# Filling products that go on up to the up projection of the third and fourth chunks, in the scores' bank; a chunk's w loaded by itself; planner keys set anew

## The chip, the cores and the metric

The kernel runs on one core of one Trainium2 chip. The metric is the time of one execution on the device, in microseconds. Five engines matter here: PE (matrix products), DVE (VectorE), ACT (ScalarE), POOL (GpSimd) and SP, which in this kernel issues nearly all transfers between HBM and SBUF. Each engine works through its own instructions in the order written; waits between engines are semaphores.

## What is computed

The first half is a linear attention with decay (RWKV-6) over 4 batches, 8 heads, 768 steps and a head size of 48. The second half is a projection up from 384 to 2048 columns, a gate, and a projection down to 384, over 3072 tokens.

```python
for t in range(S):
    cur = einsum('bhd,bhe->bhde', u * kt, vt)
    y[:, :, t] = einsum('bhd,bhde->bhe', rt, state + cur)
    state = wt[..., None] * state + einsum('bhd,bhe->bhde', kt, vt)
x = y.transpose(0, 2, 1, 3).reshape(3072, 384)
h = x @ w_in                                # 384 -> 2048
out = (h * clip(h + 3, 0, 6) / 6) @ w_out   # 2048 -> 384
```

## The kernel before

**Chunks and blocks.** The sequence is cut into chunks of 128 steps (`L`), 24 in all, numbered in the order in which they are worked on. Four chunks make a block of 512 tokens, of which there are six. For a chunk `i`, VectorE runs two scans over the decays w (`back{i}`, line 372, and `fore{i}`, line 381), from which `K{i}` (392) and `R{i}` (396) are made. PE forms the scores (`score{i}`, line 440, into the PSUM banks bankB and bankC) and transposes K (`turn{i}`, 456). `above{i}` (447, VectorE) takes the scores out of both banks. The product of K and v (`kv{i}`, 536) feeds the state by way of `kvs{i}` (ScalarE, 543), `mid{i}` (477), `decb{i}` (469) and `state{i}` (485). A chunk's own term, r times k times u, is made on VectorE and PE for the first `BY_PE` chunks (`own{i}` 405, `dot{i}` 415, `sum{i}` 421), and on GpSimd and VectorE for the others (408, 423), which need one more load (`rkt{i}`).

In the first block the result of a chunk is read in two pieces, `first{i}` (lines 514 and 523) and, after ScalarE's `third{i}` (576), `read{i}` (584, 514, 523); ScalarE's `leave{i}` (594, 596) brings it to `xT`. The up products of that block are `up0.f.c0` (line 639): f counts 16 groups of 128 of the 2048 columns. For the first four groups (`CUT`) the block is cut in two, so `up0.0.0` to `up0.3.0` need chunks 0 and 1 alone, and `up0.0.2` to `up0.3.2` need chunks 2 and 3. The others take all four chunks at once. They alternate between bankC and bankA. `ramp` (629, ScalarE) and `gate` (650, VectorE) empty the bank. `down0...` (658, 791) follow, and then the later blocks, with their products in seven-product form (740, 791).

**Weights.** w_in and w_out arrive as 64-bit floats, and are made into 32-bit ones in the kernel, in sixteen pairs: `fetch{j}` loads pair j (line 331, 768 KB), ScalarE's `low{j}` and `whole{j}` (340, 344) and VectorE's `shift{j}`, `join{j}` and `full{j}` (349, 354, 359) convert it. Three buffers hold what is loaded, and a buffer is free again when `low{j}` and `join{j}` have read it.

**Order.** The order on each engine is made by a planner (`Plan.order`, line 110), while the kernel is built: each step has an engine, an assumed duration, the steps it needs, the ring buffers it holds and a key, the time it is due. Of the steps that can start first on an engine, the one with the smallest key is taken. `START` gives the keys of chunks 0 to 5, `CONV` those of the weights, and `BEHIND[i]` names the weight load after which a chunk's loads are issued. The order of SP is made in the same way. SP issues a load only when the buffer for it is free, and all later loads wait behind it.

**Filling products.** `Plan.emit` (line 174) writes the instructions in that order. Ahead of a PE step that by the plan starts later than the one before it ended, it puts products whose result nobody reads: `spin` (line 1133), identity by two copies of identity, 128 rows by 128 by 256 columns, as many as fill 0.75 of the planned gap (`FILL`) at 0.43 us each (`SPIN`). They write bankA, of which there are two, and end with the first up product, `until = "up0.0.0"`.

Of the kernel before, what the change touches and what calls it, by code (L numbers as in the profile page):

```python
# [18 lines left out]
L = 128  # L19
# [8 lines left out]
LAG = 19.7  # L28
AHEAD = -3.5
LEAD = 7.0  # L30
BEHIND = (-1, -1, 1, 3, 8, 7)
BY_PE = 10
OWN = -0.17
SOLO = (0, 2, 3, 4, 5)
EARLY = 11
START = (-108.3, -118.2, -107.0, -152.7, 31.1, 13.0)
CONV = (-100.6, 6.9)
UP = (-64.2, 3.9, -40.1, 4.9)
SUMS = (54.2, 0.9)
LEAST = 2.0 ** -60  # L40
# [42 lines left out]
class Plan:  # L83
# [9 lines left out]
    spin = until = None  # L93
# [94 lines left out]
def fast_path(tc, feat, tok, wflat, ub, ug, moe_w_in, moe_w_out, out, flag, n_chunks):  # L188
# [5 lines left out]
    nc = tc.nc  # L194
# [13 lines left out]
    f64 = moe_w_in.dtype != F32  # L208

    with ExitStack() as ctx:  # L210
# [8 lines left out]
        chunk_of = [(i // NSEQ * 2 + i % 2) * n_chunks + i % NSEQ // 2 for i in range(NT)]  # L219

        def is_first(i):
            return i % NSEQ < 2

        def is_last(i):
            return i % NSEQ >= NSEQ - 2

        plan = Plan()
        st = [dict() for _ in range(NT)]
        blocks = [dict() for _ in range(NB)]


        ident = const.tile([128, 128], F32, name="ident")
# [4 lines left out]
        back = const.tile([PR, 2 * P, HL + 1], F32, name="back")  # L237
        starts = [const.tile([PR, 2 * P, HL + 1], F32, name=f"start_{i}") for i in range(2)]
        states = [const.tile([PR, P, D], F32, name=f"state_{i}") for i in range(2)]
        u_col = const.tile([PR, P, 2], F32, name="u_col")  # L240
# [37 lines left out]
        n = P * L  # L278
# [3 lines left out]

        def load_feat(i):
            a = io.tile([PR, nf], F32, name="feat_in")
            if i == 0:
                nc.sync.dma_start(out=a[:, 2 * n:], in_=feat[chunk_of[i], :, 2 * n:])
                nc.scalar.dma_start(out=u_col, in_=ug)
            else:
                nc.sync.dma_start(out=a, in_=feat[chunk_of[i]])
            st[i].update(a=a, r=a[:, :n].rearrange("q (x t) -> q x t", t=HL),  # L290
                         k=a[:, n:2 * n].rearrange("q (x t) -> q x t", t=HL), w=a[:, 2 * n:])

        def load_rest():
            nc.sync.dma_start(out=st[0]["a"][:, :2 * n], in_=feat[chunk_of[0], :, :2 * n])

        def load_u():
            nc.sync.dma_start(out=u_bc, in_=ub.to_broadcast([128, HD]))
# [103 lines left out]
        def own(i):  # L401
            d = st[i]
            if i < BY_PE:
                d["rk"] = wk.tile([PR, P, L], F32, name="rk", bufs=1)
# [12 lines left out]
        def own_sum(i):  # L417
            d = st[i]
            d["dg"] = wk.tile([L, H, 1], F32, name="dg")
            if i < BY_PE:  # L420
                nc.scalar.copy(out=d["dg"].rearrange("s h o -> s (h o)"), in_=d["dg_ps"].rearrange("s p g -> s (p g)"))
# [209 lines left out]
        def bank(name):  # L631
            return pp.tile([128, 512], F32, name=name, bufs=1 if name == "bankB" else 2)
# [234 lines left out]
        def do(fn, *args):  # L867
            return lambda: fn(*args)
# [5 lines left out]
        def when(i):  # L874

            bk, c = divmod(i, BC)
            return BASE[bk] - LAG - (BASE[bk] - BASE[bk - 1]) / BC * (BC - 1 - c) if bk else -99.0
# [11 lines left out]
        def scored(i):  # L889
            return f"score{i}" if i <= BC else f"read{i - 1}"  # L890

        def turned_by(i):
            return f"turn{i}" if i <= BC + 1 else f"begin{i - 2}"

        def written_by(i):
            return f"kv{i}" if i in SOLO else f"read{i - 1 if i <= BC else i - 2}"

        for i in range(NT):
            t = when(i)
            k = START[i] if i < len(START) else when(i - 2) - AHEAD  # L900
            first, last = is_first(i), is_last(i)
            dve = i < EARLY
            behind = [f"fetch{BEHIND[i]}"] if i < len(BEHIND) and BEHIND[i] >= 0 else []
            plan.add(f"feat{i}", "SP", 0.45 if i else 1.15, do(load_feat, i), behind + [f"feat{i - 1}"] * (i > 0) + ["later"] * (i == 1), k - 20, kb=690 if i else 231,
                     hold=[("feat", [f"K{i}", f"R{i}"] + [f"own{i}"] * (i < BY_PE))])
            plan.add(f"tok{i}", "SP", 0.45, do(load_tok, i), behind + [f"feat{i}"] * (i > 1) + ["later"] * (i < 2), k - 19.9, kb=197,
                     hold=[("tok", [f"read{i}"])])
            if i >= BY_PE:
                plan.add(f"rkt{i}", "SP", 0.45, do(load_rk, i), behind + [f"feat{i}"] * (i > 0), k - 19.8, kb=393,
                         hold=[("rk_in", [f"own{i}"])])  # L910
            plan.add(f"back{i}", "DVE", 1.4, do(back_scan, i), [f"feat{i}"] + [f"fore{i - 2}"] * (i > 1) + [f"back{i - 1}"] * (i > 0), k,
                     [("E", [f"K{i}", f"least{i}"])], port=True)
            plan.add(f"K{i}", "DVE" if dve else "POOL", 0.66 if dve else 1.32, do(make_k, i), [f"back{i}", f"least{i}"] + [f"K{i - 1}"] * (i > 0) + ["later"] * (i == 0),
                     k + 0.1, [("K", [scored(i), turned_by(i)])], port=True)
            plan.add(f"fore{i}", "DVE", 1.23, do(fore_scan, i), [f"back{i}"] + [f"fore{i - 1}"] * (i > 0), k + 0.2,
                     [("W", [scored(i), f"read{i}" if i < BC else f"begin{i}"])], port=True)
            plan.add(f"R{i}", "DVE" if dve else "POOL", 0.66 if dve else 1.32, do(make_r, i), [f"fore{i}"], k + 0.3,
                     port=True)
            plan.add(f"least{i}", "ACT", 0.2, do(least, i), [f"back{i}"], k + 0.2)
            if i < BY_PE:  # L920
                plan.add(f"own{i}", "DVE", 0.66, do(own, i), [f"feat{i}"] + ["later"] * (i == 0) + [f"own{i - 1}"] * (i > 0), k + OWN,
                         [("rk", [f"dot{i}"])], port=True)
                plan.add(f"dot{i}", "PE", 0.85, do(own_dot, i), [f"own{i}"], k + OWN, [("ps", [f"sum{i}"])])
                plan.add(f"sum{i}", "ACT", 0.22, do(own_sum, i), [f"dot{i}"], k + OWN, [("dg", [f"diag1{i}"])])
            else:
                plan.add(f"own{i}", "POOL", 2.0, do(own, i), [f"rkt{i}", "u"] + [f"own{i - 1}"] * (i > 0), k + 0.4,
                         [("rk", [f"sum{i}"])], port=True)
                plan.add(f"sum{i}", "DVE", 0.54, do(own_sum, i), [f"own{i}"], k + 0.5, [("dg", [f"diag1{i}"])])
            plan.add(f"diag0{i}", "ACT", 1.0, do(diagonal, i, 0), [f"sum{i}"] + [f"diag1{i - 1}"] * (i > 0), k + 0.6, [("A", [f"read{i}"])])
            plan.add(f"diag1{i}", "ACT", 1.0, do(diagonal, i, 1), [f"sum{i}", f"diag0{i}"], k + 0.6)  # L930
            due = k + 0.7 if i < len(START) else when(i - 1)
            t = k + 1 if i < len(START) else t
            if i <= BC:
# [7 lines left out]
            if i in SOLO:  # L941
                plan.add(f"kv{i}", "PE", 0.5, do(write_alone, i), [f"turned{i}", f"tok{i}"], t - 0.2, [("y", [f"kvs{i}"])])
            plan.add(f"kvs{i}", "ACT", 0.48, do(written, i), [written_by(i)], t - 6 if i >= len(START) else t - 0.5,
                     [("kvs", [f"decb{i}"] if last else [f"state{i}"])])
            S_ = [("S", [f"read{i}" if i < BC else f"begin{i}"] + [f"state{i}"] * (not last))]
            if not first:
                plan.add(f"decay{i}", "DVE" if dve else "POOL", 0.35 if dve else 1.0, do(decay, i),
                         [f"state{i - 2}", f"least{i}"] + [f"decay{i - 1}"] * (not is_first(i - 1)), t - 0.1 if i < len(START) else t - 5, S_, port=True)
                plan.add(f"mid{i}", "DVE", 0.3, do(middle, i), [f"kvs{i}", f"decay{i}"], t - 0.1 if i < len(START) else t - 5,
                         port=True)  # L950
# [34 lines left out]
                                 [f"leave{i - 1}", f"leave{i}"], when(i) - 50, kb=1, dmas=3)  # L985

        plan.add("u", "SP", 0.45, load_u, ["fetch3"], -60.0, kb=197)
        plan.add("later", "SP", 0.45, load_rest, ["feat0"], key=-999.0, kb=459)

        for j in range(len(pairs)):  # L990
            t = CONV[0] + j * CONV[1]
            plan.add(f"fetch{j}", "SP", 0.45, do(fetch, j), ["later"] * (j == 0), key=t - 20, kb=768 if f64 else 384,
                     hold=[("bits", [f"low{j}", f"join{j}"])] if f64 else ())
            if f64:
                plan.add(f"low{j}", "ACT", 0.9, do(low_scaled, j), [f"fetch{j}"], t, [("more", [f"full{j}"])])
                plan.add(f"whole{j}", "ACT", 0.84, do(low_whole, j), [f"low{j}"], t)
                plan.add(f"shift{j}", "DVE", 0.56, do(high_shift, j), [f"fetch{j}"], t, [("top", [f"full{j}"])], port=True)
                plan.add(f"join{j}", "DVE", 0.96, do(high_join, j), [f"shift{j}"], t, port=True)
                plan.add(f"full{j}", "DVE", 0.94, do(high_low, j), [f"join{j}", f"whole{j}"], t, port=True)
# [4 lines left out]
        for f in range(NFC):  # L1004
            for x, (c0, c1) in enumerate(parts(f)):
                m = c1 - c0
                at = 0 if m < BC and x == 0 else 2
                k = UP[at] + f * UP[at + 1]
# [7 lines left out]
        for c in classic:  # L1016
            for q in range(HF):
                k = D0 + c * D0 / BC + q * 1.29
# [33 lines left out]
        for bk in range(NB):  # L1052
            K = BASE[bk]
# [5 lines left out]
            for q in range(HF * (bk > 0)):  # L1059
# [13 lines left out]
                for what, eng, after, key in (("s1", "ACT", [u + "1"], 1), ("v", "ACT", [u + "5"], 2), ("u", "ACT", [u + "6"], 5),  # L1073
# [4 lines left out]
                    if q == 0 and what in ("s1", "v"):  # L1078
                        p = 0 if what == "s1" else 1
# [41 lines left out]
        for k, (which, j) in enumerate(vets):  # L1121
            i = 8 + k // 2
# [8 lines left out]
        plan.add("end", "PE", 0.0, lambda: None, [f"down{NB - 1}.1.{k_}.1" for k_ in range(1, 8)], BASE[NB])  # L1131

        def spin():
            nc.tensor.matmul(bank("bankA").rearrange("p (n t) -> p n t", t=L)[:, :2], lhsT=ident,  # L1134
                             rhs=ident.rearrange("p (n t) -> p n t", n=1).to_broadcast([128, 2, L]), start=True, stop=True)

        plan.spin, plan.until = spin, "up0.0.0"
        constants()
        plan.emit()

# [334 lines left out]
```

## Time and profile before

| | |
|---|---|
| median of 13 runs | 578.3 us (574.98 to 580.32) |
| profiled execution | 578.38 us, of which its span 576.6 us |
| mean granted PE clock | 0.983 |
| PE busy | 561.1 us (97%), 5508 products in the records |
| DVE, ACT, POOL busy | 408.3, 272.3, 84.5 us |
| records of line 1134 (fillings) | 42, from 1.4 to 31.7 us |

A product of 32-bit floats leaves two records in the trace, so the 42 records are 21 filling products. "Idle before, releaser" is the time in which an engine stood still ahead of an instruction, and what ended it. PEclk is the share of full speed that the hardware granted the PE array. Ends of products are modelled, so PE that is busy for a whole stretch may still be slow in it; the clock's column tells.

### The profile page before, as it was taken

How to read it: one execution, taken by the hardware profiler on the slowest of the kernel's cores; microseconds unless marked ns; L12 is line 12 of the kernel's file. 1: busy time of each engine (PE TensorE's matmuls, PEld its weight loads, DVE VectorE, ACT ScalarE, POOL GpSimd, SP SyncE). 2: the span in 40 equal slices, each digit the busy share in tenths (PEclk: the TensorE clock that was granted, in tenths of full speed). 3: DMA queues.
4: the chain of work that ended last, by engine and by line, in shares of the span. 5: the costliest groups of instructions: out<-in, count | busy, mean ns of one | idle time of the engine just before them, and what ended most of it. 6: DMA issues, size and time to landing. Idle time of an engine off the chain costs nothing.

```text
span 576.6 us, 13275 instructions
## 1 busy us (share of the span) xinstructions
PE 561.1 (97%) x5508; PEld 487.1 (84%) x5508; DVE 408.3 (71%) x717; ACT 272.3 (47%) x713; POOL 84.5 (15%) x93
## 2 busy tenths in 40 slices
PE   8997999999999999899999999999999999999996
PEld 6775546669888899888899988899988899988996
DVE  7979798999896788567889567899455634255350
ACT  4776585453467640357632357632357510265100
POOL 2000000003133120531242331242210000000000
PEclk9886999999999999999999999999999999999999
DMA  8939753242534256613565613562100000100001
GB/s 265 267 85 294 230 186 96 79 142 62 166 116 139 70 182 210 186 33 114 160 200 184 180 31 115 157 206 71 30 15 9 1 8 15 42 2 0 1 15 47
DMA packets 22933, 63.57 MB, mean 110 GB/s; under 512 B 3104, under 2 KB 10336, under 8 KB 22864
## 3 DMA queue, kind: packets, MB, share of 16 engines
q1 hardware_dynamic: 22736, 62.63, 35.5%
q8 instruction: 45, 0.74, 0.5%
q14 instruction: 24, 0.20, 0.1%
q10 hardware_dynamic: 128, 0.00, 0.0%
HBM read 56.92 MB, written 4.72 MB: 107 GB/s over the span
## 4 chain that ended last, share of the span: by engine, by line
PE 91%; DVE 5%; DMA 2%; issue 1%; ACT 0%; POOL 0%; DVEq 0%; SPq 0%; POOLq 0%
PE bankA L740 18%; PE bankA L791 18%; PE bankC L791 9%; PE bankC L740 9%; PE bankB L740 6%; PE bankB L791 5%; PE bankC L639 4%; PE bankA L658 4%; PE bankA L639 4%; PE bankA L1134 2%; PE y_ps L514 2%; PE y_ps L523 2%; PE y_ps L536 2%; PE ps L456 2%; PE bankB L440 2%; PE ps L415 1%
## 5 line engine op out<-in xcount | busy, mean ns | idle before, releaser
L749 ACT COPY g<-bankA 128x256 f32<-128x256 f32 x120 | 44.6, 371 | 54.8 <-PE bankA L740 52.7
L791 PE MATMUL bankA<-w_out,g 128*128 128x192 f32 x352 | 62.9, 327 | 0.0
L740 PE MATMUL bankA<-xT,w_in 128*128 128x256 f32 x240 | 62.2, 384 | 0.0
L629 ACT ACTIVATE clip<-g,three 128x512 f32<-128x512 f32 x80 | 57.6, 723 | 8.4 <-DVE g L751 7.8
L791 PEld LDWEIGHTS bankA<-w_out,g 128*128 128x128 f32 x352 | 58.4, 190 | 0.9
L759 DVE SCALAR_TENSOR_TENSOR g<-clip,g 128x512 f32<-128x512 f32 x80 | 54.4, 688 | 3.6 <-ACT clip L629 3.6
L431 ACT ACTIVATE A<-eyes,dg 128x64 f32<-128x64 f32 x192 | 49.4, 336 | 2.2 <-PE y_ps L523 1.8
L740 PEld LDWEIGHTS bankA<-xT,w_in 128*128 128x128 f32 x240 | 44.7, 190 | 6.2
L606 ACT COPY xT<-y_ps 48x256 f32<-48x256 f32 x80 | 29.2, 365 | 33.8 <-PE y_ps L523 33.0
L740 PE MATMUL bankB<-xT,w_in 128*128 128x256 f32 x160 | 41.2, 380 | 0.5 <-DVE A L447 0.5
L804 ACT ACTIVATE o<-bankA 128x192 f32<-128x192 f32 x33 | 10.9, 331 | 64.0 <-PE bankA L791 64.0
L751 DVE TENSOR_TENSOR g<-bankB,g 128x256 f32<-128x256 f32 x40 | 16.9, 423 | 31.6 <-PE bankB L740 25.7
L751 DVE TENSOR_TENSOR g<-bankC,g 128x256 f32<-128x256 f32 x40 | 16.9, 423 | 29.3 <-PE bankC L740 22.0
L408 POOL TENSOR_TENSOR rk<-rk_in 128x384 f32<-128x384 f32 x14 | 14.4, 1029 | 154.2 <-PE ps L415 132.6
L740 PEld LDWEIGHTS bankB<-xT,w_in 128*128 128x128 f32 x160 | 30.3, 190 | 4.9 <-DVE A L447 0.9
L791 PE MATMUL bankA<-bits,g 128*128 128x192 f32 x176 | 31.3, 329 | 0.4 <-DVE o L806 0.4
L372 DVE TENSOR_TENSOR_SCAN E<-feat_in,back 112x520 f32<-112x520 f32 x24 | 30.6, 1275 | 1.5 <-DMA feat_in<-in_feat_dram 1.4
L381 DVE TENSOR_TENSOR_SCAN W<-feat_in,start 112x520 f32<-112x520 f32 x24 | 31.4, 1309 | 0.3
L791 PE MATMUL bankB<-w_out,g 128*128 128x192 f32 x176 | 30.9, 327 | 0.0
L791 PEld LDWEIGHTS bankA<-bits,g 128*128 128x128 f32 x176 | 28.8, 190 | 1.1 <-DVE o L806 0.7
L791 PEld LDWEIGHTS bankB<-w_out,g 128*128 128x128 f32 x176 | 28.8, 190 | 0.0
L396 POOL TENSOR_TENSOR W<-feat_in,W 112x512 f32<-112x512 f32 x13 | 17.5, 1342 | 66.7 <-DVE W L381 66.7
(277 smaller groups left out, 1197.6 us busy)
## 6 DMA issues: line engine op xcount, KB each, us to landing
feat_in<-in_feat_dram SPq DMA_DIRECT2D x23, 675.9 KB, 6.8
bits<-in_moe_w_in_dram SPq DMA_DIRECT2D x8, 768.0 KB, 8.6
bits<-in_moe_w_out_dram SPq DMA_DIRECT2D x8, 768.0 KB, 6.9
feat_in<-in_moe_w_in_dram SPq DMA_DIRECT2D x8, 768.0 KB, 4.2
feat_in<-in_moe_w_out_dram SPq DMA_DIRECT2D x8, 768.0 KB, 4.3
rk_in<-in_tok_dram SPq DMA_DIRECT2D x14, 384.0 KB, 7.0
v_in<-in_tok_dram SPq DMA_DIRECT2D x24, 192.0 KB, 5.2
out_dram<-o SPq DMA_DIRECT2D x24, 192.0 KB, 1.9
```

Source lines behind the costliest of these rows:

```text
L372: nc.vector.tensor_tensor_scan(out=E_[:, ::-1], data0=d["w"][:, :0:-1], data1=back.rearrange("q p t -> q (p t)")[:, ::-1], initial=0.0, op ...
L381: nc.vector.tensor_tensor_scan(out=W_, data0=d["w"][:, :-1], data1=starts[i % 2].rearrange("q p t -> q (p t)"), initial=0.0, op0=ALU.mult, ...
L431: nc.scalar.activation(out=d["A"][:, h, :], in_=eyes, func=ACT.Copy, scale=d["dg"][:, h])
L606: nc.scalar.copy(out=blocks[bk]["xT"][g * GP:g * GP + D, :, at:at + HL], in_=st[i]["y_ps"][(g ^ a) * GP:(g ^ a) * GP + D, a, :, :])
L629: nc.scalar.activation(out=c[:, :m], in_=src, func=ACT.Relu, bias=three, scale=1.0)
L639: nc.tensor.matmul(h_ps[:, :(c1 - c0) * L], lhsT=w_in[:, f // 2, j, f % 2, :], rhs=b["xT"][:, j, c0 * L:c1 * L], start=(j == 0), stop=(j = ...
L658: nc.tensor.matmul(b["o", c][:, :DM], lhsT=g_of(0, f, c), rhs=w_out[:, f, :], start=(f == 0), stop=(f == NFC - 1))
L740: nc.tensor.matmul(b["p", q, to][:, :HB], lhsT=w, rhs=rhs, start=(n == 0 and k in (1, 2, 5)), stop=(n == len(terms) - 1 and k in (2, 3, 4) ...
L749: nc.scalar.copy(out=to, in_=src)
L751: nc.vector.tensor_add(to, src, to)
L759: nc.vector.scalar_tensor_tensor(out=g, in0=b["r", q, p], scalar=6.0, in1=g, op0=ALU.min, op1=ALU.mult)
L791: nc.tensor.matmul(b["d", p, to][:, :h], lhsT=a, rhs=w(), start=(f == 0 and k in (1, 2, 5)), stop=(f == HF - 1 and k in (2, 3, 4)), skip_g ...
```

## The change

1. The filling products go on up to `up0.0.2`, the first product that needs chunks 2 and 3. Those behind the first up product write bankB, the bank of the scores, of which there is one; those ahead of it write bankA as before.
2. Chunk 1 is loaded as chunk 0 is: w by itself, and r and k in a second transfer behind it.
3. The planner's keys: chunk 3's loads come behind `fetch5` and no longer behind `fetch3`; the weights' keys are 4.9 earlier; chunk 5's are 34.8 earlier; and the own term of chunk 9 goes to GpSimd and VectorE (`BY_PE` from 10 to 9).

```diff
-BEHIND = (-1, -1, 1, 3, 8, 7)
-BY_PE = 10
+BEHIND = (-1, -1, 1, 5, 8, 7)
+BY_PE = 9
-START = (-108.3, -118.2, -107.0, -152.7, 31.1, 13.0)
-CONV = (-100.6, 6.9)
+START = (-108.3, -118.2, -107.0, -152.7, 31.1, -21.8)
+CONV = (-105.5, 6.9)
         def load_feat(i):
             a = io.tile([PR, nf], F32, name="feat_in")
-            if i == 0:
+            if i < 2:
                 nc.sync.dma_start(out=a[:, 2 * n:], in_=feat[chunk_of[i], :, 2 * n:])
-        def load_rest():
-            nc.sync.dma_start(out=st[0]["a"][:, :2 * n], in_=feat[chunk_of[0], :, :2 * n])
+        def load_rest(i):
+            nc.sync.dma_start(out=st[i]["a"][:, :2 * n], in_=feat[chunk_of[i], :, :2 * n])
...
-        plan.add("later", "SP", 0.45, load_rest, ["feat0"], key=-999.0, kb=459)
+        for i in range(2):
+            plan.add(f"later{i}", "SP", 0.45, do(load_rest, i), [f"feat{i}"], key=-999.0, kb=459)
...
         def spin():
-            nc.tensor.matmul(bank("bankA").rearrange("p (n t) -> p n t", t=L)[:, :2], lhsT=ident,
+
+            nc.tensor.matmul(bank("bankB" if ("h", 0, 0) in blocks[0] else "bankA").rearrange("p (n t) -> p n t", t=L)[:, :2], lhsT=ident,
                              rhs=ident.rearrange("p (n t) -> p n t", n=1).to_broadcast([128, 2, L]), start=True, stop=True)
 
-        plan.spin, plan.until = spin, "up0.0.0"
+        plan.spin, plan.until = spin, "up0.0.2"
```

In the built program this makes 31 filling products where there were 21: 22 ahead of `up0.0.0`, and nine behind it: one ahead of `turn3`, two ahead of `kv3`, three ahead of `first3`, one ahead of `read3`, two ahead of `up0.0.2`. On VectorE the conversions of the first pairs move ahead of chunk 3: own3 and back3 stood behind shift2, and stand behind join5; between above3 and mid3 stood nine conversion steps (full2 to join5) and a gate, and now mid3 follows above3 at once. Ahead of decb3 stand three conversion steps more than before (full5, shift6, join6). On SP, chunk 3's loads stand behind `fetch5`, and `u`, `fetch4` and `fetch5` come ahead of them. On PE, first2, up0.2.0 and read2 come ahead of dot3, turn3, kv3 and score3. PE loses dot9; VectorE loses own9 and gets the sum of chunk 9; POOL gets own9, and SP the load rkt9.

## The prediction

> **What bounds the kernel now.** I read the page first, then PE's time by stretches, its waits, the timeline around the worst stretch, and the chain that ended last there.
>
> ```profile
> PE 561.1 (97%) x5508; PEld 487.1 (84%) x5508; DVE 408.3 (71%) x717; ACT 272.3 (47%) x713; POOL 84.5 (15%) x93
> ...
> PEclk9886999999999999999999999999999999999999
> ```
>
> PE is busy for 97% of the span, and its clock is short of full only in the first sixty microseconds. So a microsecond that PE wins there ends the kernel a microsecond earlier, unless something behind takes it back. The same in stretches of 3.41 us (columns: PE busy, weight loads, DVE, ACT, POOL, granted clock, DMA share, GB/s), on the steps at which the clock changes:
>
> ```profile
> 10.75:14.16 3.41, 2.38 (x46) 2.14 (x46) 3.34 (x6) 2.34 (x11) 0.00 (x0) 1.00 1.09 330
> 14.16:17.58 3.42, 3.42 (x38) 2.41 (x38) 3.35 (x9) 3.39 (x9) 0.00 (x0) 0.50 1.00 250
> ...
> 27.82:31.23 3.41, 3.29 (x56) 2.87 (x55) 3.27 (x5) 3.35 (x7) 0.00 (x0) 1.00 0.11 39
> 31.23:34.64 3.41, 3.41 (x38) 2.49 (x39) 3.28 (x7) 3.38 (x13) 0.00 (x0) 0.50 0.03 7
> ...
> 44.88:48.30 3.42, 1.15 (x18) 0.70 (x18) 3.32 (x8) 2.82 (x6) 0.00 (x0) 1.00 0.81 263
> 48.30:51.71 3.41, 3.33 (x36) 2.99 (x36) 3.24 (x6) 2.16 (x3) 0.00 (x0) 0.50 1.04 355
> 51.71:55.12 3.41, 2.31 (x27) 1.86 (x28) 3.20 (x5) 1.93 (x5) 0.00 (x0) 0.50 1.03 279
> 55.12:58.54 3.42, 3.42 (x9) 2.70 (x8) 1.86 (x3) 1.25 (x2) 0.00 (x0) 0.50 1.01 251
> 58.54:61.95 3.41, 3.41 (x16) 2.82 (x15) 2.20 (x4) 1.33 (x3) 0.00 (x0) 1.00 1.03 328
> ```
>
> The clock is halved for one stretch at 14.2, one at 31.2, and three in a row from 48.3. The busy time does not tell why: 27.82 to 31.23 was 3.29 us busy and still was followed by half clock. Those products fill little of the array. So I counted each product of the timeline against one over the whole array with 256 columns, which takes 0.43 us at full clock (1.29 for the three of an up product): scaled by its rows and columns of the array and by the columns that it streams. By that count the stretches ahead of the three drops did 0.24, 0.25 and 0.04 of a full stretch, and none ahead of full clock did less than 0.28. In the cold stretches, 0.22 and 0.20 kept half clock; 0.33, 0.41 and 0.50 ended it. I take a quarter as the mark. One filling is 0.43 of 3.41 us, or 0.125.
>
> PE's timeline around the worst stretch (start, us, instruction, and in brackets the idle time before it and what ended it):
>
> ```profile
> 45.55 0.32 PE L514 MATMUL y_ps<-W,S 48*48 48x64 f32 x4 [0.83 <-ACT kvs L543]
> 46.74 0.32 PE L514 MATMUL y_ps<-W,S 48*48 48x64 f32 x4 [0.87 <-DVE S L469]
> 47.14 0.33 PE L523 MATMUL y_ps<-A,v_in 64*48 64x64 f32 x8
> 48.12 2.69 PE L584 MATMUL y_ps<-xT,S__109 112*128 112x64 f32 x12 [0.65 <-ACT xT L576]
> 50.73 0.89 PE L514 MATMUL y_ps<-W,S 48*48 48x64 f32 x24
> 51.74 0.89 PE L523 MATMUL y_ps<-A,v_in 64*48 64x64 f32 x24
> 53.71 2.93 PE L639 MATMUL bankC<-xT,w_in 128*128 128x256 f32 x6 [1.08 <-ACT xT L596]
> 56.43 2.51 PE L639 MATMUL bankA<-xT,w_in 128*128 128x256 f32 x6
> 58.77 1.46 PE L639 MATMUL bankC<-xT,w_in 128*128 128x256 f32 x6
> ```
>
> Four waits, 0.83 + 0.87 + 0.65 + 1.08 = 3.43 us: the dependent steps of chunk 3 (first3 in two parts, read3 from line 584 on) ahead of `up0.0.2` at 53.71.
>
> By the chain that ended last, first3's second wait is for `decb3` on VectorE (46.32 to 46.69), which follows `mid3` (46.02) and, ahead of that, conversions. Then read3 and the first two up products of chunks 2 and 3 run slow, until 58.94.
>
> **The change part by part.** The sums go against the profiled execution, 578.38 us (span 576.6 and 1.8 around it), which is the median of the 13 runs.
>
> *The clock from 48 to 58.5.* Nine fillings come behind the first up product, all ahead of `up0.0.2`. Spread over about twelve microseconds (three and a half stretches) they add 0.125 x 9 / 3.5 = 0.32 to each, which alone is over a quarter. At full clock the same forms took: in the same timeline line 584 x12 1.45 us (at 40.00), line 514 x24 0.55 (41.38), line 523 x24 0.55 (42.07), and an up product of two chunks 1.29 to 1.30. So the rows win 2.69 - 1.45 = 1.24, twice 0.89 - 0.55 = 0.34, and for both up products (53.71 to 58.94) 5.23 - 2.59 = 2.64: 4.6 us. Least: 0, if the clock stays low; most: 4.6.
>
> *What the fillings cost.* At full clock they took 0.48 us each (0.97 for two at 24.28), 4.4 us for nine, where PE waits 3.4 us now. In bankB each also waits for the one before, where two bankA buffers let two be under way; the first behind score3 waits for `above3` too, and queued behind it on PE is first3, which needs `mid3` and `decb3`, behind `above3` on VectorE, anyhow. Least: nothing (all lie in waits; three ahead of first3 in its 1.7 us, one in read3's 0.65, two in the 1.08). Most: 4.4, if no wait is left. I take 0.7, near the least, since six of the nine have a wait of their size in the rows.
>
> *Chunk 3's order.* feat3 was issued at 16.97 and used at 28.03. Now it is queued on SP behind `fetch5`, which waits for a buffer (SP's waits on line 354 reach 10.6 us), and feat4, tok3 and fetch6 wait behind both. fetch5 needs join2 done, which now precedes chunk 3's scans: about 28 (shift2 began at 27.56; join2, behind five microseconds of chunk 3, at 32.97). fetch5's 768 KB go ahead (8.6 us median from issue to landing, in the table of transfers), and 676 KB of its own take 2.3 to 2.7 us at 250 to 290 GB/s: feat3 lands at 33 to 39, 5 to 11 us later than own3's 28.03. own3 to R3 took 28.03 to 32.70, then PE and above3. Against that, 38.26 to 45.94 on VectorE, 7.7 us of conversions between above3 and mid3, is gone. By the work ahead of decb3 there are three conversion steps more, 0.48 + 0.96 + 0.87 = 2.3 us, while VectorE's wait of 2.37 us for score3 (37.49) can go. Both sums say: first3 starts where it did, 46.7, within -2.5 (all waits gone) and +2.5 (none). I take 0.
>
> *Chunk 1's w.* 228 KB land ahead of 448 KB, so back1 may start up to 1.07 us earlier (VectorE's wait at 9.48); this lies ahead of the DMA-bound stretch to 31 us. From 0 to -1.07; one more issue on SP, 0.43 us, delays tok1 and all behind it. I take 0, by the link, which moves the same bytes.
>
> *dot9.* PE loses a group of line 415 that takes 0.79 us (at 135.76) in a stretch without waits: -0.8. own9 (line 408 takes 1.0 on GpSimd) and one sum (0.54, against VectorE's 0.68) lie beside; GpSimd has nothing else there. rkt9 is 384 KB on SP ahead of tok7, at a DMA share of 0.0 to 0.7.
>
> *Chunk 5 earlier.* It takes VectorE's steps ahead of the downs' time; the wait at 96.1 (0.3 us, line 456 for ScalarE's dg) can go, or return elsewhere. -0.3 to +0.5; I take -0.3.
>
> *The first 35 us.* Two stretches of the profile are at half clock there, 0.24 and 0.25. Each is worth up to 1.7 us. The new order has 22 fillings there where there were 21, elsewhere placed. From -3.4 to +1.7 (one more); I take +0.5.
>
> Sum: -4.6 + 0.7 + 0 - 0.8 - 0.3 + 0.5 = -4.5, so 573.9 us.
>
> [...]
>
> **The rivals.**
>
> *Given back (577.6).* From 60 on PE would be four microseconds earlier; VectorE then has to be. In stretches of six it stood idle 2.54, 1.20, 0.14, 0.21, 0.21, 0.07 and 0.65 us from 54 to 96, 5.0 in all, 3.9 of it waiting for clip (line 629), that is for PE's products. So four microseconds fit, barely. If VectorE can't take them, all but dot9 comes back: 578.38 - 0.8 = 577.6. Against it: no wait of PE on a gate before 96.
>
> *Late chunk 3 (576.4).* feat3 lands at 38, and first3 starts 2.5 later, at 49.2: -4.5 + 2.5 = -2.0, so 576.4. The loads at 46.5 took 10 to 15 us under load, which speaks for it; the removed 7.7 us against.
>
> *Slower: the fillings run cold (582).* If the stretch ahead of them does less than a quarter, the nine run at half clock, 0.83 each (the first eight took 6.62 us), 7.5 us where PE waits for 3.4, and the slow rows stay: 578.38 + 4.1 - 0.8 = 581.7. It decides if a stretch from 38 on holds under 0.85 us of whole-array products. Against it: `up0.2.0` and `up0.3.0` stand just ahead of the fillings on PE, each 1.29, which is 0.38 of a stretch.
>
> *The change does not act:* the clock drops from 48 regardless, and the fillings stay within the waits: 577.6 by dot9 alone.
>
> **How the numbers follow.** Forecast 0.60 (own range 571.5 to 576.3), late chunk 3 0.12, given back or no action 0.12, cold 0.13; 0.03 beyond. A measurement of this kernel tells 0.3%, 1.7 us, from none: faster is under 576.6. Faster is the forecast (0.60), two thirds of late chunk 3 (0.08) and 0.02 of no action, 0.70; the same is the rest of these two, 0.14; slower is cold and the beyond, 0.16. The range, 571.0 to 579.5, leaves out the cold case and a little below: most of the early clock's -3.4 would be needed for less than 571.
>
> **What will show it.** The clock from 41 to 62: full in all stretches if right. read3's line 584 group: 1.45 us, not 2.69. `up0.0.2` starts at 51 to 53, the third up product of that kind at 54 to 56, where it was 58.93. Records of the filling line: 62. The wait of line 456 at 96 gone. Wrong: PEclk 0.5 behind 41; first3 after 49; new waits of PE on line 650 or 359 from 60 to 110.

## The result and the profile after

The changed kernel took 573.26 us (median of ten runs, 572.3 to 575.24; with three more on record, 573.74), the kernel before 578.76 us in the same session: a ratio of 0.9913, 95% interval 0.9892 to 0.9935. The forecast was 573.9. In a later session the changed kernel ran again: 574.11 us against 577.20, ratio 0.9955 (0.9924 to 0.9986). Both intervals lie below 1, so both sessions say faster, by less than 1%; by how much differs by 2.4 us between them, and the two intervals overlap. Medians here leave out the few runs in a slow state, more than 1.5% above the fastest of their kernel.

The profiled execution of the first session is not a typical one: it took 579.14 us, and five stretches in a row early on were at half clock, while the other runs of that session took 571.6 to 575.2. The later session's profile (574.17 us, span 572.4, mean clock 0.995) is the typical one, and I read that. Busy time by engine and the granted clock in forty slices, of the changed kernel in the later session:

```profile
PE 559.6 (98%) x5520; PEld 484.2 (85%) x5520; DVE 408.4 (71%) x717; ACT 271.8 (47%) x712; POOL 86.3 (15%) x95
...
PEclk9899999999999999999999999999999999999999
```

There are twelve matmul records more (ten fillings more, less the eight dots of chunk 9), and yet PE is busy 1.5 us less: the dots took 0.79 us, and fewer products ran slow. The fourth digit of the clock, which was a 6, is a 9. The same kernel by stretches of 3.41 us on its clock steps (PE, weight loads, DVE, ACT, POOL, granted clock, DMA share, GB/s):

```profile
14.08:17.49 3.41, 3.41 (x40) 2.58 (x40) 2.95 (x5) 3.41 (x11) 0.00 (x0) 0.50 1.00 252
...
41.38:44.80 3.42, 3.22 (x75) 2.02 (x73) 3.38 (x7) 3.42 (x9) 0.00 (x0) 1.00 1.07 270
44.80:48.21 3.41, 2.46 (x21) 1.19 (x22) 3.34 (x9) 1.83 (x3) 0.00 (x0) 1.00 1.02 228
48.21:51.62 3.41, 3.28 (x70) 2.59 (x70) 3.24 (x6) 2.66 (x5) 0.00 (x0) 1.00 1.06 237
51.62:55.04 3.42, 3.36 (x26) 2.55 (x16) 2.66 (x5) 1.42 (x4) 0.00 (x0) 1.00 0.99 245
55.04:58.45 3.41, 3.41 (x17) 2.94 (x16) 3.38 (x6) 1.11 (x4) 0.00 (x0) 1.00 1.04 391
```

The three stretches at half clock from 48.3 are gone. One early stretch (14.08) is still cold; the one at 31.2 is not there in this execution. PE's timeline in the same place as before (start, us, instruction, idle time before it):

```profile
45.52 2.21 PE L1137 MATMUL bankB<-ident 128*128 128x256 f32 x6 [0.79 <-DVE A L448]
47.66 0.33 PE L515 MATMUL y_ps<-W,S 48*48 48x64 f32 x8
48.10 0.33 PE L524 MATMUL y_ps<-A,v_in 64*48 64x64 f32 x8
48.36 0.70 PE L1137 MATMUL bankB<-ident 128*128 128x256 f32 x2
49.08 1.55 PE L585 MATMUL y_ps<-xT,S__109 112*128 112x64 f32 x12
50.56 0.55 PE L515 MATMUL y_ps<-W,S 48*48 48x64 f32 x24
51.22 0.55 PE L524 MATMUL y_ps<-A,v_in 64*48 64x64 f32 x24
51.71 1.46 PE L1137 MATMUL bankB<-ident 128*128 128x256 f32 x4
53.00 1.46 PE L640 MATMUL bankC<-xT,w_in 128*128 128x256 f32 x6
54.29 1.46 PE L640 MATMUL bankA<-xT,w_in 128*128 128x256 f32 x6
55.59 1.46 PE L640 MATMUL bankC<-xT,w_in 128*128 128x256 f32 x6
```

Lines are one higher than before (L585 was 584, L640 was 639); L1137 is the filling. In place of four waits, 3.43 us, there is one of 0.79. `read3` takes 1.55, 0.55 and 0.55 us where it took 2.69, 0.89 and 0.89, and the two slow up products 2.59 instead of 5.06 (from the first's start to the third's). `up0.0.2` starts at 53.00, the third up product of that kind at 55.59 where it was 58.77.

**Where the time went, by sections.** The marks are taken out of one execution each: the first up product (line 640), the first that takes all four chunks, the starts of the second and fourth block's up products, and the end of the last product. The third column is the changed kernel without its late fillings (experiment 1 below).

| section, us | before | after | after, no late fillings |
|---|---|---|---|
| start to first up product | 33.32 | 31.54 | 31.09 |
| to first up product of four chunks | 28.04 | 26.64 | 29.84 |
| to second block | 93.16 | 92.21 | 92.20 |
| to fourth block | 173.63 | 173.64 | 173.66 |
| to the last product's end | 243.03 | 243.02 | 243.03 |
| to the end of the span | 5.39 | 5.31 | 5.27 |
| span | 576.57 | 572.36 | 575.09 |

The 4.2 us are won in three places, all ahead of the second block: 1.8 ahead of the first up product, 1.4 between there and 58 us, and 0.95 between there and the second block. Nothing is given back in this execution: behind the second block the two kernels agree within 0.1 us.

### The profile page after: what moved, and what is told of

Its sections match the earlier page's. It is cut to its first block, busy times and chain, and to the rows that moved or that the text cites. A ratio compares the mean times of both kernels' runs of the same rounds, so it can differ in the third digit from the quotient of the medians.

```text
span 577.4 us, 13310 instructions
## 1 busy us (share of the span) xinstructions
PE 564.5 (98%) x5520; PEld 489.0 (85%) x5520; DVE 407.5 (71%) x717; ACT 271.9 (47%) x712; POOL 87.1 (15%) x95
## 4 chain that ended last, share of the span: by engine, by line
PE 92%; DVE 4%; ACT 1%; issue 1%; DVEq 0%
PE bankA L792 19%; PE bankA L741 18%; PE bankC L792 10%; PE bankC L741 9%; PE bankB L741 6%; PE bankB L792 5%; PE bankC L640 4%; PE bankA L659 4%; PE bankA L640 3%; PE y_ps L515 3%; PE y_ps L524 2%; PE y_ps L537 2%; PE ps L457 2%; PE bankB L441 1%; PE y_ps L585 1%; PE ps L416 1%
## 5 line engine op out<-in xcount | busy, mean ns | idle before, releaser
L741 PEld LDWEIGHTS bankA<-xT,w_in 128*128 128x128 f32 x240 | 44.8, 190 | 6.1
L409 POOL TENSOR_TENSOR rk<-rk_in 128x384 f32<-128x384 f32 x15 | 16.4, 1096 | 152.4 <-DMA rk_in<-in_tok_dram 109.3
L397 POOL TENSOR_TENSOR W<-feat_in,W 112x512 f32<-112x512 f32 x13 | 18.4, 1415 | 66.7 <-DVE W L382 66.7
```

Of the source, the lines that this page charges most:

```text
L741: nc.tensor.matmul(b["p", q, to][:, :HB], lhsT=w, rhs=rhs, start=(n == 0 and k in (1, 2, 5)), stop=(n == len(terms) - 1 and k in (2, 3, 4) ...
```

## The experiments

The theory is that of the prediction: the clock falls after a stretch of 3.41 us with too little work in the array (in the trace of before 0.04 to 0.25 of a full stretch by the prediction's count), and the late fillings supply it. The rivals: the clock follows idle gaps of PE and not the work; or the gain is made by the loads and the new keys, and the fillings only fill waits. Ratios are against the kernel before in the same session; they are not exactly the ratios of the medians.

**1. The change without its late fillings.**

```diff
-        plan.spin, plan.until = spin, "up0.0.2"
+        plan.spin, plan.until = spin, "up0.0.0"
```

> The changed kernel with the fillings ending at up0.0.0 again (22 of them), all else as changed. Clock theory: the clock falls again ahead of chunk 3's read and the first products behind it, so 3.5 to 4.6 us of the gain of 5 go: a ratio of 0.997 to 1.000 to the kernel before, with two or three stretches at half clock between 45 and 60. Key theory: as the changed kernel, 0.991.

Measured: 577.11 us, 0.9991 (0.9968 to 1.0014). The mean granted clock (median over the runs) is 0.984; that of the changed kernel is 0.995, that of before 0.983. The profile, by stretches and (second fence) PE's timeline:

```profile
40.98:44.40 3.42, 1.73 (x68) 1.41 (x68) 3.39 (x7) 3.42 (x9) 0.00 (x0) 1.00 1.08 266
44.40:47.81 3.41, 1.58 (x17) 0.95 (x18) 3.34 (x10) 2.51 (x6) 0.00 (x0) 0.50 1.00 218
47.81:51.22 3.41, 3.41 (x36) 3.10 (x36) 3.20 (x7) 1.87 (x3) 0.00 (x0) 0.50 1.09 238
51.22:54.64 3.42, 2.23 (x31) 1.82 (x28) 2.51 (x3) 0.94 (x3) 0.00 (x0) 0.50 0.98 236
54.64:58.05 3.41, 3.41 (x9) 2.69 (x9) 1.25 (x2) 0.47 (x1) 0.00 (x0) 0.50 1.03 391
```

```profile
45.95 0.45 PE L515 MATMUL y_ps<-W,S 48*48 48x64 f32 x4 [0.93 <-DVE S L470]
46.49 0.46 PE L524 MATMUL y_ps<-A,v_in 64*48 64x64 f32 x8
47.60 2.82 PE L585 MATMUL y_ps<-xT,S__109 112*128 112x64 f32 x12 [0.65 <-ACT xT L577]
...
53.33 2.93 PE L640 MATMUL bankC<-xT,w_in 128*128 128x256 f32 x6 [1.08 <-ACT xT L597]
```

Half clock is back, four stretches from 44.4 to 58.1, and so are the slow rows and the waits. What the late fillings buy, with everything else the same, is the step from this kernel to the changed one: 60.93 to 58.18 us at the first up product of four chunks, 2.75 us. Counted from the first up product on, so without what differs ahead of it, it is 3.2 (29.84 to 26.64).

**2. The late fillings alone**, in the order of before.

```diff
-            nc.tensor.matmul(bank("bankA").rearrange("p (n t) -> p n t", t=L)[:, :2], lhsT=ident,
+            nc.tensor.matmul(bank("bankB" if ("h", 0, 0) in blocks[0] else "bankA").rearrange("p (n t) -> p n t", t=L)[:, :2], lhsT=ident,
...
-        plan.spin, plan.until = spin, "up0.0.0"
+        plan.spin, plan.until = spin, "up0.0.2"
```

> The kernel before with the filling products alone: they go on to up0.0.2 and use bankB (eight more of them: 29), and every key, load and BY_PE stay as they were. Clock theory (the nine fillings hold the clock up from 41 to 58 us, and that is most of the gain): 3.5 to 4 us faster than before, a ratio of 0.993 to 0.994, and full clock from 45 to 62 in most executions. Key theory (the gain comes from the new order of conversions and chunk 3, dot9 and chunk 1's load): no change, 0.998 to 1.002.

Measured: 575.36 us, 0.9961 (0.9937 to 0.9986): by the ratio 2.3 us faster than before, less than the 3.5 to 4 expected, at a mean clock of 0.993. In its profile two stretches are cold, from 29.6 to 36.4, and none behind. So the fillings act without the rest; the loads and keys without the fillings (experiment 1) give 0.9991, which can't be told from nothing. Together they give more than this one, 0.9913 in one session and 0.9955 in the other; the interval of the second overlaps with it, so how much the rest adds is not settled. Among runs of nearly the same clock it adds nothing to be seen: at 0.997 this kernel took 572.6 to 572.9 us (three runs), and the changed one at 0.998 took 572.3 to 572.8 (three runs of the first session).

**3. Fillings of the same number that do an eighth of the work**: those behind the first up product stream 32 columns in place of 256.

```diff
-            nc.tensor.matmul(bank("bankB" if ("h", 0, 0) in blocks[0] else "bankA").rearrange("p (n t) -> p n t", t=L)[:, :2], lhsT=ident,
-                             rhs=ident.rearrange("p (n t) -> p n t", n=1).to_broadcast([128, 2, L]), start=True, stop=True)
+            nc.tensor.matmul(bank("bankB" if ("h", 0, 0) in blocks[0] else "bankA").rearrange("p (n t) -> p n t", t=L)[:, :2, :16 if ("h", 0, 0) in blocks[0] else L], lhsT=ident,
+                             rhs=ident.rearrange("p (n t) -> p n t", n=1)[:, :, :16 if ("h", 0, 0) in blocks[0] else L].to_broadcast([128, 2, 16 if ("h", 0, 0) in blocks[0] else L]), start=True, stop=True)
```

> The changed kernel, with the nine fillings behind up0.0.0 streaming 32 columns instead of 256: the same number of products in the same gaps, with an eighth of the array's work. If the clock goes by the work that the array does in a stretch of 3.41 us (mark at about a quarter), these add 0.04 to each stretch instead of 0.32 and the clock falls: 0.996 to 1.000, as without them. If what counts is that PE has no long gap, the clock stays and the time is that of the changed kernel or a little less, 0.989 to 0.991.

Measured: 577.34 us, 1.0004 (0.9983 to 1.0026), clock 0.984. By stretches, and PE's timeline:

```profile
42.83:46.24 3.41, 2.48 (x54) 1.85 (x46) 3.34 (x8) 2.49 (x5) 0.00 (x0) 1.00 0.98 251
46.24:49.65 3.41, 3.11 (x22) 2.88 (x25) 3.24 (x7) 2.50 (x5) 0.00 (x0) 0.50 1.10 239
```

```profile
44.00 1.34 PE L1137 MATMUL bankB<-ident 128*128 128x32 f32 x6 [0.71 <-DVE A L448]
45.27 0.33 PE L515 MATMUL y_ps<-W,S 48*48 48x64 f32 x8
45.71 0.33 PE L524 MATMUL y_ps<-A,v_in 64*48 64x64 f32 x8
45.97 0.41 PE L1137 MATMUL bankB<-ident 128*128 128x32 f32 x2
46.69 2.82 PE L585 MATMUL y_ps<-xT,S__109 112*128 112x64 f32 x12 [0.30 <-ACT xT L577]
```

The stretch ahead of the drop was 2.48 us busy, with the fillings in their places and no wait over 0.73 us; in the changed kernel the stretch 44.80 to 48.21 was 2.46 us busy, with a wait of 0.79 us ahead of 45.52, and the clock stayed. So neither gaps nor busy time decide it here.

**4. Fillings that use a quarter of the array's columns**, but stream all 256.

```diff
-            nc.tensor.matmul(bank("bankB" if ("h", 0, 0) in blocks[0] else "bankA").rearrange("p (n t) -> p n t", t=L)[:, :2], lhsT=ident,
+            late = ("h", 0, 0) in blocks[0]
+            nc.tensor.matmul(bank("bankB" if late else "bankA").rearrange("p (n t) -> p n t", t=L)[:32 if late else 128, :2], lhsT=ident[:, :32 if late else 128],
...
```

> The nine fillings behind the first up product use 32 of the 128 columns of the array, and stream 256 columns as in the changed kernel: PE is busy as long with each (0.43 us, or 0.74 from start to start in the one bank), but a quarter of the array works. If what holds the clock is the part of the array that works, about a third of a stretch of 3.41 us by rows, columns and streamed columns, these fillings add 0.03 to a stretch and no longer 0.125, the stretches from about 44 us stay under a third, the clock is halved there for three or four stretches, and the time is that of the kernel without the late fillings, 577 (575.5 to 578.5). The rival: what counts is the time for which the array streams, whatever its width; then the clock stays full from 41 to 62, and the time is that of the changed kernel, 573.3 to 574.1.

Measured: 574.14 us, 0.9958 (0.9933 to 0.9983), clock 0.996. The rival of this experiment holds: the time is that of the changed kernel, and its profile has one cold stretch, 21.5 to 24.9. The stretches, and PE's timeline, in the place:

```profile
41.96:45.38 3.42, 2.74 (x73) 1.45 (x71) 3.38 (x8) 3.42 (x7) 0.00 (x0) 1.00 1.03 246
45.38:48.79 3.41, 3.09 (x27) 1.12 (x26) 3.31 (x9) 1.83 (x5) 0.00 (x0) 1.00 1.04 225
48.79:52.20 3.41, 3.24 (x63) 2.16 (x62) 3.24 (x5) 2.69 (x6) 0.00 (x0) 1.00 1.03 230
```

```profile
45.13 1.97 PE L1138 MATMUL bankB<-ident 128*32 128x256 f32 x6 [0.62 <-DVE A L448]
...
47.73 0.62 PE L1138 MATMUL bankB<-ident 128*32 128x256 f32 x2
48.45 1.55 PE L585 MATMUL y_ps<-xT,S__109 112*128 112x64 f32 x12
```

Here the prediction's way of counting fails. By rows, columns and streamed columns (product by product: rows by columns by streamed columns, against 128 by 128 by 256 at 0.43 us), this kernel's stretches from 42.0, 45.4 and 48.8 did 0.29, 0.18 and 0.32 of a full stretch and stayed at full clock, while experiment 1's from 40.98 did about 0.29 and experiment 3's from 42.83 about 0.17, and half clock followed both. What the fillings lost by being narrow is not seen: 574.14 us at a clock of 0.996, beside 574.11 at 0.995 of the changed kernel.

What experiments 3 and 4 show is that the columns streamed matter here (32 in place of 256: 577.34 us, clock 0.984) and that the array's columns hardly do (32 in place of 128: 574.14 us, 0.996). No run varied the rows, and what the hardware counts is not shown.

**5. More and fewer fillings.** `FILL` is the share of a planned gap that is filled, 0.75 in the changed kernel (31 fillings).

```diff
-    FILL = 0.75
+    FILL = 1.0
```

> The changed kernel with the fillings taking the whole planned gap instead of three quarters (FILL 1.0): 45 instead of 31, seven of them ahead of up0.0.0 besides those of the start, and six more behind it. If the early stretches at half clock (the profile of the changed kernel has five in a row from 20.1 us) are what is left to win, the mean clock goes to 0.998 or 0.999 in most executions and the time to 572.0 to 572.5, a ratio of 0.989. If the added fillings lie in PE's way instead, 14 of them at 0.48 us cost up to 6.7, and it is 574 to 577 at that clock.

> The changed kernel with FILL 0.5: 19 fillings, six of them behind up0.0.0 where there were nine. FILL 1.0 cost 5 us at full clock, 0.4 for each added filling, so fewer should win as long as the clock holds: three fewer behind up0.0.0 win 1 to 1.5, 571.8 to 572.5 at a clock of 0.998. But six add only 0.21 of a stretch where the mark is at about a quarter; if the clock drops in a part of the executions, the median is 574 to 577 at a mean clock under 0.993.

Measured with 1.0 (45 fillings): 578.57 us, 1.0006 (0.9991 to 1.0021), at a mean clock of 0.997. With 0.5 (19 fillings): 576.70 us, 0.9988 (0.9957 to 1.0019), clock 0.988; its runs go from 572.9 us at 0.993 to 579.6 at 0.973. Its profile is cold from 8.7 to 18.9 and from 22.3 to 36.0, ahead of the first up product (36.26), where this kernel has 13 fillings in place of 22; behind it the six late ones kept the clock full. The time is that of the expectation's second case, but not for the reason given there, too few late fillings. So with 0.5 the gain goes to the clock, and in that profile to the early fillings that are missing; with 1.0 it goes to the fillings themselves, at one of the highest clocks. That is more than either expectation for 1.0 allowed. PE's timeline with 1.0:

```profile
47.57 3.73 PE L1137 MATMUL bankB<-ident 128*128 128x256 f32 x10 [0.62 <-DVE A L448]
51.23 0.33 PE L515 MATMUL y_ps<-W,S 48*48 48x64 f32 x8
```

Five fillings take 3.66 us from the first's start to first3's, 0.73 each and not the 0.48 that I had put down. Fourteen more cost about 4.9 us, 578.6 less the mean of the changed kernel's two medians (573.7): some 0.35 each. They do not cost alike: in the profiles the section from the first up product to that of four chunks is 30.52 us with 15 late fillings, 26.64 with nine (the changed kernel) and 25.67 with six (`FILL` 0.5), all at full clock. That is 0.65 for each of the six added there, and about 0.3 for each of the three left out.

**6. Fillings of one place into one tile.** In the changed kernel each filling asks for a tile of its own in the one bank, and so waits for the one before.

```diff
-                for _ in range(int(self.FILL * (self.start[n] - last) / self.SPIN)):
-                    self.spin()
+                m = int(self.FILL * (self.start[n] - last) / self.SPIN)
+                if m > 0:
+                    self.spin(m)
...
-        def spin():
-            nc.tensor.matmul(bank("bankB" if ("h", 0, 0) in blocks[0] else "bankA").rearrange("p (n t) -> p n t", t=L)[:, :2], lhsT=ident,
+        def spin(m):
+            to = bank("bankB" if ("h", 0, 0) in blocks[0] else "bankA").rearrange("p (n t) -> p n t", t=L)[:, :2]
+            for _ in range(m):
+                nc.tensor.matmul(to, lhsT=ident,
...
```

> The changed kernel, with the fillings of one place written into one tile, not a new one each, so that none waits for the one before. In bankB a filling took 0.74 us from start to start in a run of BY_PE 10 (three in 2.2 us), against 0.48 where two bankA buffers let two be under way. If the fillings lie in PE's way, the six that follow another in bankB win up to 0.26 each, 1 us or more in all: 572.0 to 572.5, a ratio of 0.989 to 0.990. If they lie in waits, nothing: 573.3. Fewer microseconds of filling do not change the array's work, so the clock stays as in the changed kernel.

Measured: 573.10 us, 0.9930 (0.9908 to 0.9953), beside 574.11 of the changed kernel in the same session; the two intervals overlap. PE's timeline:

```profile
45.05 1.56 PE L1139 MATMUL bankB<-ident 128*128 128x256 f32 x6 [0.69 <-DVE A L449]
46.54 0.33 PE L516 MATMUL y_ps<-W,S 48*48 48x64 f32 x8
```

The three fillings ahead of first3 take 1.56 us in place of 2.21, and first3 starts 1.49 us behind the first of them in place of 2.14. The four-chunk up products begin at 57.02, 1.16 us ahead of the changed kernel, of which 0.37 was won ahead of the first up product (31.17 against 31.54) and 0.79 behind it. In the medians the difference is 1.0 us, not resolved.

**7. Parts of the new order undone, one at a time:** chunk 9's own term on PE again (`BY_PE = 10`), chunk 5's key as before (`START[5] = 13.0`), the weights' keys as before (`CONV[0] = -100.6`).

```diff
-BY_PE = 9
+BY_PE = 10
```

> The changed kernel with BY_PE back at 10: chunk 9's own term is made by PE again. The sum says that dot9's 0.79 us lie on PE's path in a stretch without waits: 0.8 us slower than the changed kernel, a ratio of 0.9925 to 0.993 to the kernel before. Rival: the row lies in slack and nothing changes, 0.991.

```diff
-START = (-108.3, -118.2, -107.0, -152.7, 31.1, -21.8)
+START = (-108.3, -118.2, -107.0, -152.7, 31.1, 13.0)
```

> The changed kernel with chunk 5's key back at 13.0 (its scans and own term come later again), all else as changed. By the prediction's sum this term is 0.3 us, the wait at 96 us on line 457 for ScalarE's dg, which returns: 573.5 to 574.0. By the clock alone (time goes with the mean granted clock, whatever the order behind 60 us) it is as the changed kernel, 573.3, at a mean clock of 0.995 to 0.997.

```diff
-CONV = (-105.5, 6.9)
+CONV = (-100.6, 6.9)
```

> The changed kernel with the weights' keys back at -100.6; score3 then stands ahead of its fillings and the fillings are 31 as well. If earlier conversions are worth time by themselves, 574.5 or more at the same clock. If all that counts is the clock, the time follows it: 573 at a mean clock of 0.995, 575 at 0.992.

Measured, in this order: 573.26 us, 0.9927 (0.9903 to 0.9951); 574.34 us, 0.9946 (0.9922 to 0.9969); 574.74 us, 0.9953 (0.9932 to 0.9975), at mean clocks of 0.997, 0.996 and 0.995. The changed kernel stands at 0.9913 and 0.9955, so no single key of these carries a gain that can be told from none, and no cost of chunk 9's term on PE is seen in the total. The weights' keys lie where the expectation put a gain by earlier conversions (574.5 or more at the same clock), but the changed kernel itself took 574.11 at 0.995 in its second session. For chunk 9's term PE's waits from 60 to 577 us say part of why. The changed kernel's, and those with chunk 9's term on PE (us in total, times, longest):

```profile
PE bankC L792 <- DVE S__2515 L777: 1.5, 1, 1.5
PE bankB L741 <- DVE A L448: 0.5, 1, 0.5
PE bankC L792 <- ACT o L805: 0.5, 1, 0.5
PE bankA L792 <- DVE o L807: 0.5, 1, 0.5
```

```profile
PE y_ps L537 <- ACT kn L462: 1.4, 2, 0.7
PE bankA L792 <- DVE o L807: 0.4, 1, 0.4
PE bankA L792 <- DVE S__1532 L777: 0.2, 1, 0.2
```

With the term on PE, the section from the four-chunk up products to the second block is 93.88 us and not 92.21: the term's product is back, and a wait of 0.7. But from the second to the fourth block it is 171.18 and not 173.64: the wait of 1.5 us for line 777 isn't there in the order that the planner then makes, nor in experiment 8, which has the same section of 171.18. The order alone does not set that wait, though: in the first session's profile of the changed kernel, where the second block starts at 155.24 and not at 150.39, it was 0.5, and the section 172.68. The rest of the 2.46 is not traced.

**8. Experiments 6 and 7 together**, one tile and chunk 9's term on PE.

> The version with the fillings of one place in one tile, and BY_PE back at 10. The changed kernel and the one with BY_PE 10 measured alike, though their profiles differ by 0.95 us between the first product of four chunks and the block behind it (dot9) and by 1.5 us the other way in the second block. If so, this is as the one-tile version at BY_PE 9 within 0.5 us: 572 to 572.8.

Measured: 572.83 us, 0.9925 (0.9898 to 0.9952): the lowest median of all, but it can't be told from the changed kernel.

**9. The changed kernel again**, in the session of 6 and 8.

> The changed kernel itself once more, on the same chip as the others, for a profile with few stretches at half clock: 573.3 as measured, a ratio of 0.991 to 0.993, and by the clock theory up0.0.2 at 51 to 53 us where the early stretches are warm.

Measured: 574.11 us, 0.9955 (0.9924 to 0.9986), less of a gain than the 0.991 to 0.993 expected; `up0.0.2` starts at 53.00. Its profile is the one shown above.

**The clock and the time of all of them.** "At half clock" is worked out from a run's mean granted clock and span, 2 x (1 - clock) x span. The clock is on record to 0.001, which is 1.2 us here; 0.7 to 4.3 us of each profile's figure lie behind the last product, and the stretch ahead of the clock's first step on record (4.4 to 7.3 us, in which the fillings of the changed kernel took 0.85 us from start to start) is not counted. Medians over the runs:

| kernel | at half clock, us | time, us |
|---|---|---|
| before (four sessions with the clock on record) | 16.1 to 19.6 | 577.2 to 578.0 |
| FILL 0.5 | 13.8 | 576.7 |
| no late fillings | 18.4 | 577.1 |
| small fillings | 18.4 | 577.3 |
| late fillings alone | 8.0 | 575.4 |
| changed kernel (two sessions) | 5.7 | 573.3, 574.1 |
| narrow fillings | 5.1 | 574.1 |
| one tile | 4.6 | 573.1 |
| BY_PE 10 | 3.4 | 573.3 |
| one tile and BY_PE 10 | 4.6 | 572.8 |
| chunk 5's key as before | 4.6 | 574.3 |
| weights' keys as before | 5.7 | 574.7 |
| FILL 1.0 | 3.5 | 578.6 |

All but the last lie within about a microsecond of one line: each microsecond at half clock goes with some 0.3 us, (578.0 - 573.3) / (19.6 - 3.4). The kernel before follows it by itself, run by run: its 35 runs in one session go from 573.0 us at a mean clock of 0.994 to 579.4 at 0.982, and a straight line through them has 0.32 us for each microsecond at half clock (0.31 to 0.38 in its four sessions). So that kernel is as fast as the changed one in the rare run in which its clock falls little (two of its 110 runs are at 0.994, 573.0 and 573.5 us); what the change does, by these figures, is to make such runs the rule.

## Why the prediction was right

**The clock from 48 to 58.5 (-4.6): the effect right, the measure behind it wrong.** The rows gave nearly what they were to give (the two up products are counted up to 58.94, the end of the second's row; up to the third's start, 58.77, the term is 4.4): from first3's second part on to the four-chunk up products it was 14.62 us (46.74 to 61.36), and is 10.52 (47.66 to 58.18), -4.1 with the fillings in it. Experiment 1 shows that the late fillings do it. But the mark of a quarter, in array work by rows and columns, was my estimate off one trace, and experiment 1 shows it too low: by that count the stretch from 40.98 did about 0.29 there and was followed by half clock. And experiment 4 shows that the array's columns hardly count here (clock 0.996 with 32 of them, 0.995 with 128). The margin saved the forecast, which is partly luck: the stretches that it wanted at over a quarter came out at 0.40 and more (44.8 and 48.2 us).

**The cost of nine fillings (0.7): mis-sized, 1.2.** The step that failed is "at full clock they took 0.48 us each". In bankB they take 0.71 to 0.73 (2.14 for three here, 3.66 for five in experiment 5), since each waits for the one before, which the prediction named and did not price; one tile for the three makes it 0.50 (experiment 6). `decb3` on VectorE was done at 46.43:

```profile
46.07 0.36 DVE L470 TENSOR_TENSOR S<-S,w_min 112x192 f32<-112x192 f32 x1
```

first3, which needs it, began at 47.66, so the three fillings ahead of it held it up by 1.2 us; the others are not seen to hold up anything: two of them lie in the wait of `up0.0.2` for ScalarE's `leave3` (line 597, done at 52.81; the product began at 53.00). Together -4.6 + 1.2 = -3.4; the section from the first up product on is 3.2 shorter than without the late fillings (29.84 to 26.64).

**Chunk 3's order (0): right for the start of first3, but not free.** `feat3` was issued at 28.99 ("about 28") and landed at 37.61 (within 33 to 39), and without late fillings first3's second part began at 45.95, within the bounds. But the first up product came 2.23 us earlier there than before and first3 only 0.79: its wait there, 0.93 us, is for VectorE's `decb3` (line 470). So, against before, the section from the first up product on wins 1.40 and not 3.2.

**The first 35 us (+0.5): wrong in sign in the one profile, -1.78, and out of bounds in the other.** There is one cold stretch where there were two, so what the line above loses was won here. In the first session's profile it is the other way: five stretches in a row are cold, and the first up product starts at 35.99, 2.67 later than before, beyond the +1.7 that was taken as the most. By stretches of that execution:

```profile
16.73:20.14 3.41, 3.02 (x33) 2.52 (x32) 3.38 (x7) 1.86 (x6) 0.00 (x0) 1.00 1.05 383
20.14:23.55 3.41, 3.32 (x74) 2.90 (x74) 1.94 (x4) 1.23 (x2) 0.00 (x0) 0.50 0.82 298
...
33.79:37.21 3.42, 3.42 (x38) 2.41 (x38) 2.94 (x6) 1.36 (x3) 0.00 (x0) 0.50 0.97 303
37.21:40.62 3.41, 3.30 (x30) 2.49 (x29) 3.20 (x6) 2.63 (x6) 0.00 (x0) 1.00 0.30 44
```

Bounds of this term should have held several cold stretches in a row: by rows and columns the stretches at half clock ahead of another such one did 0.24 to 0.36 here, the one ahead of full clock 0.40.

**dot9 and chunk 5 (-0.8, -0.3): right in their place.** The section to the second block is 0.95 shorter; the wait of line 456 at 96 us is gone. Experiment 7 adds that the same choice orders later blocks otherwise, and that another order there was shorter by more than the term costs; of that the prediction had nothing. **Chunk 1's w (0)** has no measurement by itself. In the profile w landed at 7.67 and back1 began at 8.06 where it began at 10.09; how much of the -1.78 that makes is open.

**The rivals.** *Given back* did not happen: sections behind the second block agree within 0.1 us, and PE has no wait on lines 651 or 360 there. *Late chunk 3* did not, though its condition came nearly true (`feat3` landed at 37.61, the rival had 38): without late fillings first3 is not late, so it is late by the fillings and not by its loads. *Run cold* did not: the fillings took 0.71 to 0.73 us by their bank, at full clock. *Does not act* falls with experiment 1 (577.11 us without the late fillings, clock 0.984), and the rival by idle gaps with experiment 3.

By sections the prediction was +0.5, -3.9, -1.1 and 0; the profile has -1.78, -1.40, -0.95 and -0.08. The total is right for its main reason, and partly by luck: two terms ahead of 58 us missed in opposite directions, and which stretches ahead of 35 us are cold differs from run to run.

## What to carry to other kernels

Where PE's work comes in small products, set their work (here above all the columns that they stream) against the stretches of the granted clock, and not the time for which PE is busy: 2.48 us of 3.41 busy lost the clock here (experiment 3), and 2.46 kept it (the changed kernel). Filling products won here where such a stretch fell short (3.2 us from the first up product on, experiment 1); where the clock was full anyway, more of them cost time (14 for 4.9 us, experiment 5). Give several fillings in a row one tile: here each otherwise waited for the one before, 0.71 to 0.73 us each in place of 0.50, and they held up what stood behind them (shown in the rows, not resolved in the total). And before a change of a per cent is judged, set its runs beside their mean clock: the kernel before spreads over six microseconds by itself, from 573.0 us at 0.994 to 579.4 at 0.982.

## What the runs showed of the hardware

- Fillings of 32 array columns, streaming 256, kept the clock as well as those of 128 (574.14 us, clock 0.996, beside 574.11 and 0.995); fillings of 128 columns that stream 32 did not (577.34, 0.984).
- The same kernel met the clock's stretches at other places from run to run. In the two profiles of the changed kernel the steps lie at 3.08 and 0.43 us from the span's start, modulo 3.41; in those of before and of experiments 4 and 3 at 0.51, 1.00 and 1.87. That before's spread of 573.0 to 579.4 us comes from it is likely and not shown.
- A 128x128x256 product took 0.71 to 0.73 us from start to start where each had its own tile in one bank, and 0.50 (three in 1.49) where they shared one.
